# Order of one GpSimd multiply and two others in the steps that begin a row of chunks: gated linear attention followed by a mixture of experts, on one core

## The chip, the cores and the metric

The kernel runs on one core of one Trainium2 chip. The metric is the device time of one execution in microseconds (us). A core has five instruction streams that run beside each other and wait for one another by semaphores: TensorE (PE; its weight loads are shown as PEld), VectorE (DVE), ScalarE (ACT), GpSimd (POOL) and SyncE (SP, which here issues most of the DMA transfers). Each stream is worked off in the order in which it was written.

## The reference

The first half is a recurrence over 768 time steps for 4 batches and 8 heads of width 48; its rows are then routed to one of 8 experts each, a two-layer network with a ReLU, weighted by the gate.

```python
for t in range(S):
    state = alpha[:, :, t, :, None] * state + np.einsum('bhd,bhe->bhde', k[:, :, t], v[:, :, t])
    y[:, :, t] = np.einsum('bhd,bhde->bhe', q[:, :, t], state)
...
expert_idx = np.argmax(logits, axis=1)
...
h = np.maximum(x_sorted[lo:hi] @ w1[e], 0.0)
y_sorted[lo:hi] = h @ w2[e]
...
return (gate_w[:, None] * y).astype(np.float32)
```

## The kernel before

Time is cut into 6 chunks of 128 steps. One tile is one chunk of one batch: 24 tiles, numbered s = 4 * chunk + batch (`B` is 4). A step of the main loop (line 669, `for i in range(-4, NT)`) works on several tiles at once: it scores tile i, prepares the operands of tile i + 2, transposes those of tile i + 1, and projects tile i - 1. The whole loop stands under a manual schedule, so every engine runs its instructions in the order in which this loop writes them.

What a step writes, with the names and lines used below:

- **Loads** (`loads_for`, line 379): SP fetches a, k, q and v of later tiles, in pairs of tiles from step 2 on.
- **Scores** (line 461, PE) of tile i, then in steps 4, 8, 12, 16 and 20 `decay_cols` (line 429, PE): it transposes the row `er`, the decay that lies between two chunks, and DVE copies it to a tile `E` (line 431).
- **Masks** (line 469, DVE), **transposes** (line 448, PE) of tile i + 1, which read the tile `kqb`, **sums** (line 392, PE) with the two exponentials `icp` and `cp` (lines 395 and 396, ACT) of a tile further on.
- **Decay rows**: ACT issues small transfers of rows of `icp` and `cp` (line 409). In the steps before 4, 8, 12, 16 and 20 POOL makes `er` from them (lines 417 and 418).
- **`operands(i + 2)`** (line 438, POOL): two multiplies, k times `icp` and q times `cp`, into one of three tiles `kqb`. The tile is used again after `keys_values` (line 509, PE) of the tile before has read it.
- **`scale_state`** (line 476, POOL): the decayed state `U`, which is the state of the same batch one chunk earlier times `E`. In a step with i % 4 = 0 the state of tile i and that of tile i + 1 are both made there. In other steps only that of tile i + 1 is, except in the last of a row, where `decay_rows` stands in its place.
- **One-hots** (lines 290 and 291): the routing of earlier tiles, a pair of instructions for each tile, on POOL in steps 13, 14, 16, 19, 20 and 21 for tiles 0 to 10 and 13, and on DVE for others.
- **`read_state`** (line 488, PE) of tile i reads `U` of tile i; then `attend` (line 498), `keys_values` (line 509) and the projection `rows` of tile i - 1 (line 535), all PE. `rows` writes a PSUM tile `x` that ACT reads in `keep_rows` (line 560).
- In step 21, between `attend` and `rows`, PE sums up the routing of tiles 0 to 15 with 16 small matmuls, one for each tile in order (`tokens`, line 298). Their result is decoded on DVE and starts a gather on POOL (line 639) for the first expert rows.

After the loop the experts run one after another, with PE nearly without a gap.

Every transfer signals its completion on one of eight counters, and a transfer is not issued before the one that used its counter last has landed; which counter each takes is decided when the program is built.

Of the kernel before, what the change touches and what calls it, by code (L numbers as in the profile page):

```python
# [18 lines left out]
def kernel(  # L19
# [268 lines left out]
    def one_hots(eng, *tiles):  # L288
        for s in tiles:
            eng.tensor_scalar(oh_r[:, s, :], iota_r[:], scalar1=rc[:, 0, s : s + 1], scalar2=None, op0=ALU.is_equal)  # L290
            eng.tensor_scalar(
                oh_c[:, s, :], iota_c[:], scalar1=rc[:, 1, s : s + 1], scalar2=tokv[:, s : s + 1],
                op0=ALU.is_equal, op1=ALU.mult,
            )

    def tokens(tok_ps, *tiles):
        for s in tiles:
            nc.tensor.matmul(
                tok_ps, lhsT=oh_r[:, s, :], rhs=oh_c[:, s, :], start=(s == 0), stop=(s == NT - 1), skip_group_check=True,
            )  # L300
# [62 lines left out]
    with tc.tile_pool(name="ld", bufs=6) as ld, \  # L363
# [21 lines left out]
        def logs(s):  # L385
            t = work.tile([C, Dm], F32, name="lna", bufs=4)
            nc.scalar.activation(t[:], st[s]["a"].rearrange("s h d -> s (h d)"), AF.Ln)
            st[s]["lna"] = t

        def cums(s, bank="cum"):  # L390
            cum = ps.tile([C, 512], F32, name="cum", tag=bank)
            nc.tensor.matmul(cum[:, :Dm], lhsT=cum_m[:], rhs=st[s]["lna"][:], start=True, stop=True)  # L392
            cp = work.tile([C, Dm], F32, name="cp", bufs=6)
            icp = work.tile([C, Dm], F32, name="icp", bufs=6)
            nc.scalar.activation(icp[:], cum[:, :Dm], AF.Exp, scale=-1.0)
            nc.scalar.activation(cp[:], cum[:, :Dm], AF.Exp)  # L396
            st[s]["cp"], st[s]["icp"] = cp, icp

        def decay_out(s, which=(0, 1)):
            c, b = cb(s)  # L400
            cp, icp = st[s]["cp"], st[s]["icp"]


            for j in which:
                cc, row = ((c, icp[0:1, :]), (c + 1, cp[C - 1 :, :]))[j]
                if 0 < cc < NB:
                    if cc not in decay:
                        decay[cc] = work.tile([B, 2, Dm], F32, name="dec", bufs=3)
                    nc.scalar.dma_start(decay[cc][b : b + 1, 1 - j, :], row)
            if b == 0 and c + 1 < NB and 1 in which:  # L410
                alpha0[c + 1] = work.tile([B, H, D], F32, name="alpha0", bufs=3)
                nc.sync.dma_start(alpha0[c + 1][:], alpha[:, :, (c + 1) * C, :])

        def decay_rows(c):
            t = by_half(er[:B])
            d = decay[c].rearrange("b i (a p d) -> b i a p d", a=2, p=NP)
            nc.gpsimd.tensor_tensor(t, d[:, 0], d[:, 1], op=ALU.mult)
            nc.gpsimd.tensor_tensor(t, t, alpha0[c].rearrange("b (a p) d -> b a p d", a=2), op=ALU.mult)
# [7 lines left out]
        def decay_cols(c):  # L426
            ep = ps.tile([C, NP, C], F32, name="ep", tag="cum")
            for p in range(NP):
                nc.tensor.transpose(ep[:, p, :], pair(er[:], p), ident[:])
            decay[c] = work.tile([C, NP, B], F32, name="E", bufs=2)  # L430
            nc.vector.tensor_copy(decay[c][:], ep[:, :, :B])
# [82 lines left out]
        def result(s):  # L514
            d = st[s]
            d["yT"] = work.tile([C, 2, 2, C], F32, name="yT")
            nc.scalar.copy(d["yT"][:], y[:, :, : 2 * C].rearrange("r g (j t) -> r g j t", j=2))  # L517
# [46 lines left out]
        def do(f, i, *a):  # L564
            if 0 <= i < NT:
                f(i, *a)
# [7 lines left out]
        def new_sums(i):  # L574
            return range(sums_to(i - 1) + 1, sums_to(i) + 1)
# [9 lines left out]
        def loads_for(i):  # L585
            for n in singly.get(i, ""):
                load_next(n, 1)
            if i > 1:
                for n, upto in ("a", sums_to(i + 4)), ("v", i + 3), ("k", i + 5), ("q", i + 5):
                    while loaded[n] <= min(upto, NT - 1):  # L590
                        load_next(n, 2)
# [22 lines left out]
        def early_turn():  # L614
            t = ld.tile([C, 2, H, D], F32, name="k_sb", bufs=3)
            eg["xT"] = t.rearrange("p b h d -> p (b h d)").rearrange("p (a t) -> p a t", a=DB)
            for j in range(EARLY // C):
                tp = ps.tile([C, DB, C], F32, name="tp", bufs=2)
                for a in range(DB):
                    nc.tensor.transpose(tp[:, a, :], eg["xg"][:, j, a * C : (a + 1) * C], ident[:])  # L620
                nc.scalar.copy(eg["xT"][:, :, j * C : (j + 1) * C], tp[:])
# [11 lines left out]
        def early_gather():  # L633

            d = decode(held["tok"][:, : EARLY // C], EARLY // C, "e")
            gi = next(d)
            eg["xg"] = ld.tile([C, 2, H, D], F32, name="a_sb", bufs=4).rearrange("p j h d -> p j (h d)")
            for j in range(EARLY // C):
                nc.gpsimd.indirect_dma_start(
                    out=eg["xg"][:, j, :], out_offset=None,  # L640
                    in_=x_d[: (NG - 1) * TG * C, :], in_offset=bass.IndirectOffsetOnAxis(ap=gi[:, j : j + 1], axis=0),
                )
            return d
# [19 lines left out]
        def route(i):  # L663
            for f, *args in on_vector.get(i, ()):
                if f is slots:
                    args[1] = counted(args[1])
                f(*args)

        for i in range(-4, NT):
            loads_for(i)  # L670
            do(scores, i)
            if i < NT - 1:
                do(result, i - 1)
            do(logits, i - 2)
            if i >= B:
                do(add_state, i - 1)
            do(gate, i - 2)
            if i > 0:
                for s in new_sums(i):
                    logs(s)  # L680
            if i == NT - 1:
                early_turn()
            if 0 < i < NT and i % B == 0:
                decay_cols(i // B)
            do(mask, i, 0)
            do(mask, i, 1)
            if i < B:
                do(add_state, i - 1)
            do(transposes, i + 1)
            sums = list(new_sums(i))  # L690
            for s in sums[:1]:
                cums(s)
            if i < 0:
                for s in sums[1:]:
                    cums(s, "x")
            do(gate_weight, i - 2)
            route(i)
            do(keep_rows, i - 2)
            if len(sums) == 1:
                decay_out(sums[0])  # L700
            if i == -1:
                for s in range(2):
                    decay_out(s)

            if B - 1 <= i < 2 * B - 1:
                decay_out(i + 1, (1,))
            if i == NT - 2:
                si = next(se)[1]
                eg["si"] = lambda j, r: si[:r, j : j + 1]
            do(operands, i + 2)  # L710
            if i % B == 0:
                do(scale_state, i)
            if 0 < i + 1 < NT and (i + 1) % B == 0:
                decay_rows((i + 1) // B)
            elif i >= 0:
                do(scale_state, i + 1)
            one_hots(nc.gpsimd, *on_gpsimd.get(i, ()))
            do(read_state, i)
            do(attend, i)
            if i == NT - 2:  # L720
                result(i)
            if i >= 0 and sums[1:]:
                cums(sums[1])
                for s in sums:
                    decay_out(s, (0,) if i else (0, 1))
            do(keys_values, i)
            if i == NT - 3:
                held["tok"] = ps.tile([C, NC], F32, name="tok", tag="cum")
                tokens(held["tok"][:], *range((NG - 1) * TG))
                se = early_gather()  # L730
            do(rows, i - 1)
            if i in counts_in:
                counts(counts_in[i], counted(i - 1))
            if i < 0:
                for s in new_sums(i + 1):
                    logs(s)
            if i == -3:
                second_consts()
            if i in (-4, 0, 1):
                for j in {-4: (0, 1, 2), 0: (3,), 1: (4,)}[i]:  # L740
                    late_consts(j)
            if 12 <= i < 22:
                fetch_part(groups[0], i - 12)
# [515 lines left out]
```

## Time and profile before

| | us |
|---|---|
| median of 3 runs | 417.67 (416.52 to 418.47) |
| the profiled execution | 418.46 |
| its span, first to last instruction | 416.7 |
| PE busy | 404.7 (97%) |
| DVE busy | 208.8 (50%) |
| ACT busy | 171.2 (41%) |
| POOL busy | 144.2 (35%) |
| mean granted TensorE clock | 0.992 |

A share of the span says how long an engine had an instruction in it, not that it was needed that long. The loop with the 24 tiles fills the first third of the span, the experts the rest. A step takes about 5.45 us, one that begins a row of chunks about 5.9 us.

### The profile page before, as it was taken

To read this page: it belongs to the slowest core of one execution; us is meant where nothing else is said; L and a number is where in the kernel's file an instruction comes from. 1 tells how busy PE (TensorE), PEld (TensorE's weight loads), DVE (VectorE), ACT (ScalarE), POOL (GpSimd) and SP (SyncE) were. 2 spreads that over 40 slices of the span, in tenths; PEclk is the share of its full clock that TensorE was granted. 3 is DMA by queue.
4 is the path that set the end of the run, shared out by engine and by line. 5 is a ranking of instruction groups with operands and counts; after the bars stand their busy time and mean duration, and the time that the engine had idled before them with its cause. 6 is when DMAs were issued, how large, how long until landed. Compare 5 with 4: busy or idle time off the path is not lost.

```text
span 416.7 us, 9225 instructions
## 1 busy us (share of the span) xinstructions
PE 404.7 (97%) x3525; PEld 342.3 (82%) x3525; DVE 208.8 (50%) x644; ACT 171.2 (41%) x453; POOL 144.2 (35%) x193
## 2 busy tenths in 40 slices
PE   7997999999999999999999999999999999999994
PEld 4676888888888885999699889979979979979962
DVE  4552556464565575645743663463573573553200
ACT  4573565566655531134225414513513513523510
POOL 5545364678668204604002511320330230200101
PEclk9998999999999999999999999999999999999998
DMA  9999699889874316764405235155154263200101
GB/s 175 191 207 234 135 232 221 186 190 208 196 196 128 110 40 235 259 217 149 166 2 190 87 146 171 42 208 168 42 209 134 75 206 112 95 1 20 33 20 35
DMA packets 120098, 59.08 MB, mean 142 GB/s; under 512 B 102934, under 2 KB 114287, under 8 KB 120052
## 3 DMA queue, kind: packets, MB, share of 16 engines
q1 hardware_dynamic: 114932, 48.80, 45.3%
q0 software_dynamic: 3424, 9.59, 6.6%
q8 instruction: 29, 0.48, 0.5%
q10 hardware_dynamic: 1696, 0.08, 0.3%
q14 instruction: 17, 0.14, 0.1%
HBM read 48.95 MB, written 9.58 MB: 140 GB/s over the span
## 4 chain that ended last, share of the span: by engine, by line
PE 91%; issue 5%; ACT 1%; POOL 1%; DVE 1%; ACTq 0%; POOLq 0%
PE pA L884 11%; PE pB L884 9%; PE pC L957 8%; PE pA L942 7%; PE sA L461 6%; PE y L498 6%; PE tp L448 6%; PE cum L392 4%; PE pC L884 4%; PE x L535 4%; PE pB L942 4%; PE y L488 3%; PE pA L1096 3%; PE pC L942 2%; PE tp L800 2%
## 5 line engine op out<-in xcount | busy, mean ns | idle before, releaser
L979 POOL DMA_INDIRECT out_dram<-zo,sp x25 | 27.0, 1081 | 169.8 <-ACT zo L978 114.7
L184 DVE TENSOR_TENSOR h_sb<-pB,u 128x208 f32<-128x208 f32 (+6 forms) x56 | 20.1, 360 | 60.9 <-PE pB L884 44.9
L828 ACT COPY u<-pA 128x208 f32<-128x208 f32 (+6 forms) x68 | 21.6, 318 | 54.0 <-PE pA L942 50.3
L438 POOL TENSOR_TENSOR kqb<-k_sb,icp 128x384 f32<-128x384 f32 x23 | 23.0, 1002 | 42.5 <-PE y L509 21.0
L957 PE MATMUL pC<-h_sb,w 128*128 128x416 f32 (+5 forms) x96 | 32.9, 496 | 0.0
L884 PE MATMUL pA<-t,s 128*128 128x208 f32 (+6 forms) x112 | 28.6, 337 | 0.6
L461 PE MATMUL sA<-qT,kT 48*128 48x128 f32 x192 | 27.7, 284 | 0.9 <-DVE qT L452 0.9
L790 POOL DMA_INDIRECT xg<-x_rows,gp x25 | 25.9, 1036 | 7.6 <-issue 5.8
L957 PEld LDWEIGHTS pC<-h_sb,w 128*128 128x128 f32 x96 | 18.1, 190 | 12.0 <-issue 4.4
L461 PE MATMUL sB<-qT,kT 48*128 48x128 f32 x192 | 27.7, 285 | 0.0
L884 PE MATMUL pA<-xgT,w 128*128 128x208 f32 (+6 forms) x112 | 27.7, 329 | 0.0
L461 PEld LDWEIGHTS sA<-qT,kT 48*128 48x128 f32 x192 | 23.1, 187 | 3.8 <-ACT kT L454 1.1
L448 PE MATMUL tp<-ident,kqb 128*128 128x128 f32 x192 | 26.1, 279 | 0.0
L542 DVE TENSOR_REDUCE lgn<-x 128x8 f32<-128x32 f32 x23 | 4.4, 191 | 41.6 <-PE x L535 36.7
L448 PEld LDWEIGHTS tp<-ident,kqb 128*128 128x128 f32 x192 | 20.9, 141 | 3.3 <-issue 1.1
L884 PE MATMUL pB<-t,w 128*128 128x208 f32 (+6 forms) x112 | 23.4, 331 | 0.3 <-DVE h_sb L184 0.3
L438 POOL TENSOR_TENSOR kqb<-q_sb,cp 128x384 f32<-128x384 f32 x23 | 23.1, 1006 | 1.0 <-ACT cp L396 0.9
L897 ACT ACTIVATE h_sb<-h_sb 128x416 f32<-128x416 f32 (+6 forms) x28 | 14.8, 530 | 20.4 <-DVE h_sb L184 20.4
L884 PE MATMUL pC<-xgT,w 128*128 128x208 f32 (+6 forms) x112 | 23.1, 329 | 0.0
L461 PEld LDWEIGHTS sB<-qT,kT 48*128 48x128 f32 x192 | 23.1, 187 | 0.0
L469 DVE TENSOR_TENSOR dA<-sA,cmask 128x512 f32<-128x512 f32 x24 | 16.5, 689 | 11.4 <-PE sB L461 11.3
L517 ACT COPY yT<-y 128x512 f32<-128x512 f32 x24 | 14.1, 586 | 19.0 <-PE y L509 14.6
(252 smaller groups left out, 967.2 us busy)
## 6 DMA issues: line engine op xcount, KB each, us to landing
w<-in_moe_w_dram SPq DMA_DIRECT2D x14, 1536.0 KB, 7.5
x_rows<-xs SPq DMA_DIRECT2D x24, 192.0 KB, 3.8
v_sb<-in_v_dram SPq DMA_DIRECT2D x10, 384.0 KB, 5.4
k_sb<-in_k_dram SPq DMA_DIRECT2D x9, 384.0 KB, 6.7
q_sb<-in_q_dram SPq DMA_DIRECT2D x9, 384.0 KB, 6.2
a_sb<-in_alpha_dram SPq DMA_DIRECT2D x8, 384.0 KB, 4.7
a_sb<-in_alpha_dram SPq DMA_DIRECT2D x8, 192.0 KB, 4.0
w<-in_moe_w_dram SPq DMA_DIRECT2D x6, 256.0 KB, 3.0
```

Source lines behind the costliest of these rows:

```text
L184: eng.tensor_tensor(out, a, b, op=ALU.add)
L392: nc.tensor.matmul(cum[:, :Dm], lhsT=cum_m[:], rhs=st[s]["lna"][:], start=True, stop=True)
L438: eng.tensor_tensor(by_half(kq[:, i]), d[n].rearrange("s (a p) d -> s a p d", a=2), d[e][:].rearrange("s (a p d) -> s a p d", a=2, p=NP), ...
L448: nc.tensor.transpose(tp[:, p, :], pair(kqb[s % 3][:, i], p), ident[:])
L461: nc.tensor.matmul(t[:, p, :], lhsT=d["kT"][r : r + D, p, :], rhs=d["qT"][r : r + D, p, :], start=True, stop=True,)
L498: nc.tensor.matmul(yv(g)[o : o + D, j, :], lhsT=d["v"][:, g * NP + p, :], rhs=d["d" + "AB"[g]][:, p, :], start=(s < B and j == 0), stop=Tr ...
L790: nc.gpsimd.indirect_dma_start(out=g["xg"][:r, j, :], out_offset=None, in_=x_d[:, :], in_offset=bass.IndirectOffsetOnAxis(ap=g["gi"](j, r) ...
L828: nc.scalar.copy(t[:, :m], bank["A"][:, :m])
L884: nc.tensor.matmul(out, lhsT=ops[n_][0], rhs=ops[n_][1], start=first and n_ == names[0], stop=True, skip_group_check=True,)
L942: nc.tensor.matmul(out, lhsT=lhs, rhs=rhs, start=first and f == 0, stop=True, skip_group_check=True)
L957: nc.tensor.matmul(d2[:, :n], lhsT=w2[:, f, 2 * C :], rhs=h[:, f, :n], start=(f == 0), stop=(f == FB - 1),)
L979: ins = nc.gpsimd.indirect_dma_start(out=out[:, :], out_offset=bass.IndirectOffsetOnAxis(ap=g["si"](j, r), axis=0), in_=zo[:r], in_offset= ...
```

## The change

One line of the loop moves by two lines. In steps 4, 8, 12, 16 and 20 POOL ran both multiplies of `operands(i + 2)`, then `U` of tile i and `U` of tile i + 1. Now `U` of tile i stands first, then the two multiplies, then `U` of tile i + 1. In step 0 `scale_state` does nothing, since there is no earlier chunk, and in all other steps nothing moves.

```diff
             if i == NT - 2:
                 si = next(se)[1]
                 eg["si"] = lambda j, r: si[:r, j : j + 1]
-            do(operands, i + 2)
             if i % B == 0:
                 do(scale_state, i)
+            do(operands, i + 2)
             if 0 < i + 1 < NT and (i + 1) % B == 0:
                 decay_rows((i + 1) // B)
             elif i >= 0:
                 do(scale_state, i + 1)
             one_hots(nc.gpsimd, *on_gpsimd.get(i, ()))
```

In the built programs no instruction is added or taken away on any engine, and the order on PE, DVE, ACT and SP is the same. Two things differ beside the order on POOL. The semaphore that a `read_state` of such a step waits for now comes with the first `U` and no longer after the operands; the transposes of the next tile get a wait of their own for the operands. And from step 4 on the transfers take other completion counters than before, so that a load or a decay row can wait for another transfer than it did.

## The prediction

> **What bounds the kernel.** I read the slices first.
>
> ```profile
> PE   7997999999999999999999999999999999999994
> ...
> PEclk9998999999999999999999999999999999999998
> ```
>
> PE is busy nearly everywhere; slice 4 (31.3 to 41.7 us) is the one after the start with a dent, and the granted clock dips in the same slice. Next, PE's waits, longest first:
>
> ```profile
> PE y L488 <- POOL U L476: 2.5, 1, 2.5
> ```
>
> Columns: microseconds in total, times, longest. PE's largest wait in the whole span is one wait of `read_state` for `U`. The view of PE's weight loads shows five such waits, 5.0 us, the longest 3.1, but the load queue runs ahead: in steps 8, 12, 16 and 20 the matmuls have no gap. So what counts is step 4. POOL there, by its timeline (start, length, engine, line, what; in brackets the idle time before it and its releaser):
>
> ```profile
> 34.10 1.00 POOL L438 TENSOR_TENSOR kqb<-k_sb,icp 128x384 f32<-128x384 f32 x1 [1.37 <-DMA k_sb<-in_k_dram]
> 35.96 0.99 POOL L438 TENSOR_TENSOR kqb<-q_sb,cp 128x384 f32<-128x384 f32 x1 [0.86 <-ACT cp L396]
> 36.91 0.99 POOL L476 TENSOR_TENSOR U<-acc,E 128x192 f32<-128x192 f32 x2
> ```
>
> and PE:
>
> ```profile
> 34.15 0.81 PE L392 MATMUL cum<-lna,cum_m 128*128 128x384 f32 x2
> 37.48 0.65 PE L488 MATMUL y<-qT,U 48*48 48x128 f32 x16 [2.52 <-POOL U L476]
> ```
>
> Both multiplies of tile 6 wait for loads: k by the releaser named; q, I take it, also, since the `cp` of tile 6 was made two steps earlier (the `cp` that ended at 35.93 is tile 9's) and its load, issued at 30.36 with a median landing of 6.2 us, was due about then. `U` of tile 4, whose `E` DVE finished at 33.65, stands behind them. After the gap PE runs slowly. The windows (length, then busy time of PE, PEld, DVE, ACT and POOL; last three columns granted clock, DMA share, GB/s):
>
> ```profile
> 37.50:41.80 4.30, 4.30 (x66) 3.96 (x66) 0.00 (x0) 0.59 (x1) 1.50 (x3) 0.60 1.24 234
> ```
>
> In windows of half a microsecond the clock is 0.50 from 38.5 to 41.5 and 1.00 again from 42.0.
>
> **What step 4 gains.** `U` of tile 4 can start as soon after `E` as in step 8 (60.08 to 60.17, 0.09): at 33.74, and ends at 34.26 (row median 0.518). PE is then still in its transposes and sums, so `read_state` follows the sums as elsewhere, 0.74 behind their start (60.59 to 61.33): 34.89 in place of 37.48, which is 2.59 us. From there to the next scores step 8 takes 61.33 to 64.01 = 2.68 us at full clock, step 4 took 37.48 to 41.79 = 4.31: another 1.63. Together **4.22 us**. As a check: from scores to scores step 4 took 31.64 to 41.79 = 10.15, step 8 58.13 to 64.01 = 5.88, a difference of 4.27.
>
> [...] The row shows half clock 0.7 us after that gap, for some 3.4 us. [...]
>
> What is late next? `rows` of tile 3 would stand at 34.89 + 1.85 (61.33 to 63.18) = 36.74; it needs `x`, which ACT's `keep_rows` frees at 36.40 (35.82 + 0.58): 0.34 to spare. The transposes of tile 6 come 1.09 after the scores (64.01 to 65.10), at 38.7; its q multiply still starts with the load at 35.96 and ends at 36.95. `U` of tile 5 ends at 37.4 and is read at 40.4. None of these takes the gap's place.
>
> **Steps 8, 12 and 16.** [...] POOL in step 8 now:
>
> ```profile
> 57.62 1.00 POOL L438 TENSOR_TENSOR kqb<-k_sb,icp 128x384 f32<-128x384 f32 x1 [0.30 <-issue]
> 58.58 1.01 POOL L438 TENSOR_TENSOR kqb<-q_sb,cp 128x384 f32<-128x384 f32 x1
> 60.17 0.99 POOL L476 TENSOR_TENSOR U<-acc,E 128x192 f32<-128x192 f32 x2 [0.59 <-DVE E L431]
> ```
>
> The operands fill the time in which POOL would wait for `E`. With `U` first POOL idles until 60.17, and behind it the operands end at 60.17 + 0.50 + 1.92 = 62.59 in place of 59.58, 3.01 later. [...] The rows say who waits: the transposes of tile 10 start at 65.10, 2.51 later. The second `U` ends at 63.09, read at 66.77. The next operands (63.51) wait for PE anyway, and POOL had 2.35 us idle there. Cost 0. Step 12 has the same offsets (`U` 82.93, operands to 85.35, transposes 87.87, next operands 86.27). In step 16 two tiles of one-hots follow (2.13 us), so the next operands start at 110.20 instead of 108.50; their transposes stand at 116.07, and POOL's idle 3.00 before 113.93 takes the delay up. Cost 0. If those covers were gone, each step would cost up to its 3.0 less whatever is left.
>
> **Steps 20 and 21** have no such cover:
>
> ```profile
> 125.90 1.00 POOL L438 TENSOR_TENSOR kqb<-q_sb,cp 128x384 f32<-128x384 f32 x1
> 127.27 0.99 POOL L476 TENSOR_TENSOR U<-acc,E 128x192 f32<-128x192 f32 x2 [0.37 <-DVE E L431]
> ...
> 130.37 1.00 POOL L438 TENSOR_TENSOR kqb<-k_sb,icp 128x384 f32<-128x384 f32 x1
> 131.32 1.02 POOL L438 TENSOR_TENSOR kqb<-q_sb,cp 128x384 f32<-128x384 f32 x1
> 132.28 0.53 POOL L476 TENSOR_TENSOR U<-acc,E 128x192 f32<-128x192 f32 x1
> 132.78 0.65 POOL L290 TENSOR_SCALAR oh_r<-iota_r,rc 128x128 f16<-128x128 f16 x1
> 133.41 0.48 POOL L291 TENSOR_SCALAR oh_c<-iota_c,rc,tokv 128x32 f16<-128x32 f16 x1
> ```
>
> From 127.27 to 133.89 POOL has no gap. The operands of tile 22 (1.92) now fall behind the first `U`, so all that follows is 1.92 later: operands of tile 22 done at 129.69 (transposes 131.26, fine), `U` of tile 21 at 130.19 (read at 132.29, fine), operands of tile 23 at 134.2 (transposes 136.34, fine), `U` of tile 22 at 134.7 (read 137.36, fine), but the one-hots of tile 13 at 135.8. PE wants them here:
>
> ```profile
> 133.88 0.56 PE L298 MATMUL tok<-oh_c,oh_r 128*128 128x32 f16 x16
> ```
>
> Tile 13 is the fourteenth of these: 133.88 + 13 * 0.033 = 134.31. PE stops until 135.87: **1.55 us lost**. Everything behind (projection, decode, gather, next steps) hangs on PE's order or on this sum and shifts with it. Bounds: 0 if POOL packs tighter, 1.55 + 1.63 = 3.2 if the stall brings half clock as in step 4. [...]
>
> **The transfers.** Counters change from step 4 on, so waits for landed transfers change. The tightest I find: ACT's row of `icp` in step 6 now waits for the q load of tiles 8 and 9, issued at 37.80, largest landing 6.9: 44.7, against 50.69 - 4.2 = 46.5 when ACT gets there. In return the k load of tiles 10 and 11, held until 50.73 by a decay row, is freed. k of tiles 12 and 13 waits for a decay row issued at about 51.9 (56.12 - 4.2): + 3.6 + 6.7 = 62.2, its multiply 64.7. Cost 0; from below nothing to gain, since PE waits for no load after step 4; from above the 4.2 could be handed back. The ten added waits of the transposes: the row is the 51 ns semaphore instruction, 14 times before `read_state` with no gap on PE; 0, at most 10 * 0.05 = 0.5.
>
> **Sum.** -4.22 + 1.55 = -2.67. The profiled execution, 418.46 (span 416.7 and 1.8 around it), goes to 415.8. It is 0.79 above the median 417.67; taken from that, 415.0. The spread of the three runs, 1.95, is about a clock dip, so some may lack it, and a run without it gains less but starts lower. I take 415.3, 0.57% under the median.
>
> **The rivals.**
> - *As summed*, 0.55: 415.3.
> - *No stall in step 21*, 0.13: 417.67 - 4.2 = 413.5. For: POOL's spans are rough. Against: POOL is packed for 6.6 us there.
> - *Half the clock's part is missing*, 0.24: the median run had no dip, or step 21 gets one: -2.6 + 1.55 = -1.05 or -4.2 + 3.2 = -1.0, so 416.7. [...] Against: two of three runs sit high.
> - *Loads take the gain back*, 0.08, the other side: with step 4 shorter, the DMA-bound start (share 1.24, 234 GB/s) or a counter holds a load of steps 6 to 11 until PE waits for it. Price: one for one beyond the slack of 1.8 us at ACT and some 4 at the transposes; it decides once 4.2 is handed back and the stall stays: 417.67 + 1.55 = 419.2, more if it comes twice. For: SP issues of 1.4 to 2.9 us until 42. Against: share 0.5 from 42 to 46.
> - *The change does nothing* is ruled out: POOL's order differs in five places.
>
> About 0.5% (2.1 us) is what a measurement of this kernel can tell from no change. Faster: most of the first and the second, 0.61; within: the third and the edges, 0.33; slower: the tail of the fourth, 0.06. The range 413.3 to 417.1 holds the first three.
>
> **What would show it.** PE's wait for `U` of 2.5 gone, slice 4 of PE and clock at 9, step 4 at about 5.9 us; POOL idle for `E` some 2 to 3 us in steps 8, 12, 16, 20 with no gap on PE; a new PE wait at L298 for POOL's one-hots near 1.5. A wait of PE for a load, or a clock under 1.00 after step 21, would make me wrong.

## The result, and the profile after

| | before | after |
|---|---|---|
| median of 12 runs, us | 417.62 (416.21 to 418.47) | 416.62 (415.39 to 418.75) |
| ratio, 95% interval | | 0.9982 (0.9962 to 1.0001) |
| the profiled execution, us | 418.46 | 415.39 |
| its span, us | 416.7 | 413.7 |
| mean granted TensorE clock | 0.992 | 0.997 |

By the medians the change gains 1.0 us, 0.24%, which the interval does not separate from nothing. A gain of 0.57% was forecast. The two profiled executions are 3.07 us apart, close to the 2.67 of the sum, but by luck: the one of before is the second highest of its twelve runs, and the one of after the lowest of its twelve. That is the first thing to see here: the trace that the sum was read from was not a typical one. Here and below, ratios leave out runs more than 1.5% above the fastest of their kernel (two of e2, one of e3), while medians hold all runs.

The slices of after, beside the dent in slice 4 of before:

```profile
PE   7999999999998999999999999999999999999994
...
PEclk9999999999999999999999999999999999999998
```

The dent is gone, in PE and in the clock. A new one stands in PE's slice 13. PE's waits of after (us in total, times, longest) name it:

```profile
PE tok L298 <- POOL oh_c L291: 1.4, 1, 1.4
```

The wait for `U` is off the list. POOL's timeline of after, step 4 first (start, length, engine, line, what; in brackets the idle time ahead and its releaser):

```profile
33.46 0.51 POOL L476 TENSOR_TENSOR U<-acc,E 128x192 f32<-128x192 f32 x1 [1.00 <-DVE E L431]
34.04 1.00 POOL L438 TENSOR_TENSOR kqb<-k_sb,icp 128x384 f32<-128x384 f32 x1
35.64 1.00 POOL L438 TENSOR_TENSOR kqb<-q_sb,cp 128x384 f32<-128x384 f32 x1 [0.61 <-DMA q_sb<-in_q_dram]
...
122.77 0.51 POOL L476 TENSOR_TENSOR U<-acc,E 128x192 f32<-128x192 f32 x1 [2.27 <-DVE E L431]
...
130.71 0.47 POOL L291 TENSOR_SCALAR oh_c<-iota_c,rc,tokv 128x32 f16<-128x32 f16 x1
```

In step 4 `U` no longer stands behind the q multiply, which still waits for its load until 35.64. In step 20 POOL now idles 2.27 us for `E`, and the queue behind it ends with the one-hot of tile 13 in step 21, at 131.18. PE's timeline of after, in steps 4 and 21:

```profile
34.62 0.65 PE L488 MATMUL y<-qT,U 48*48 48x128 f32 x16
...
129.39 0.49 PE L298 MATMUL tok<-oh_c,oh_r 128*128 128x32 f16 x13
131.24 0.23 PE L298 MATMUL tok<-oh_c,oh_r 128*128 128x32 f16 x3 [1.36 <-POOL oh_c L291]
```

`read_state` has no gap ahead of it (2.52 us before), and the token sums stop ahead of tile 13 for 1.36 us. So both halves of the sum are in the trace. What they are worth in other executions is what the experiments had to find.

### The profile page after: what moved, and what is told of

It reads as the page before. It is cut to its first block, busy times and chain, and to the rows that moved or that the text cites. A ratio compares the mean times of both kernels' runs of the same rounds, so it can differ in the third digit from the quotient of the medians.

```text
span 413.7 us, 9238 instructions
## 1 busy us (share of the span) xinstructions
PE 402.2 (97%) x3525; PEld 340.5 (82%) x3525; DVE 213.2 (52%) x644; ACT 171.1 (41%) x453; POOL 143.7 (35%) x193
## 4 chain that ended last, share of the span: by engine, by line
PE 86%; issue 6%; POOL 4%; ACT 2%; DVE 1%; DMA 0%; POOLq 0%; ACTq 0%
PE pA L884 11%; PE pB L884 9%; PE pC L957 8%; PE pA L942 8%; PE sA L461 5%; PE tp L448 5%; PE y L498 5%; PE pC L884 4%; PE pB L942 4%; PE cum L392 4%; PE x L535 4%; PE pA L1096 3%; PE pC L942 2%; PE y L488 2%; PE tp L800 2%
## 5 line engine op out<-in xcount | busy, mean ns | idle before, releaser
L187 DVE TENSOR_TENSOR th<-h_sb,th 128x208 f32<-128x208 f32 (+5 forms) x48 | 17.4, 363 | 7.9 <-ACT h_sb L897 7.9
```

The costliest lines, as they stand in the source:

```text
L187: eng.tensor_tensor(out, a, b, op=ALU.subtract)
```

## The experiments

The runs fall in three groups of four kernels, each group on one chip. The kernel before took 420.82 us (median of 35 runs) in the first group, 417.28 (29) in the second, 421.39 (29) in the third. Ratios are to the runs of before in the same group.

The reading used throughout is a table: from PE's timeline of each trace, the time from the first score product of step 4 to that of step 10. In steps without any wait this stretch takes 33.55 us, as it does in e8 (steps of 5.88, 5.45, 5.44, 5.45, 5.88 and 5.45). What is above that is lost to waits and to half clock.

| trace | PE's wait for `U` in step 4 | half clock after it | step 4 to step 10 | lost |
|---|---|---|---|---|
| before | 2.52 | yes | 37.82 | 4.27 |
| before, e1 | 1.84 | no | 35.82 | 2.27 |
| old order in step 4, e4 | 2.10 | no | 35.71 | 2.16 |
| before, e12 | 2.14 | yes | 37.33 | 3.78 |
| old order, decay rows moved, e11 | 1.89 | yes | 37.10 | 3.55 |
| after | 0 | no | 33.59 | 0.04 |
| after, e2 | 0 | no | 34.50 | 0.95 |
| new order in step 4, e3 | 0 | no | 35.03 | 1.48 |
| new order, e5 | 0 | no | 34.37 | 0.82 |
| new order, e9 | 0 | no | 34.66 | 1.11 |

The table leaves out what PE loses ahead of step 4. That matters for the old order, since a PE that comes late to step 4 can wait less there: step 3 took 5.83 us in e1 and 6.16 in e4, in the other traces 5.23 to 5.73. From the first scores of step 0 to those of step 10 the five traces of the old order take 59.56 us in the mean, the five of the new 56.96.

### e1 and e2: both kernels again

No edit.

> The kernel before, unchanged, for a second trace of it. Theory A (the sum of the prediction holds in every execution): PE waits again about 2.5 us for U in step 4 and runs at half clock after it, mean granted clock 0.992. Theory B (the profiled execution was an extreme one: PE comes to step 4 earlier or later while the load that U stood behind lands at a time of its own, so that the wait swallows what the start lost): the wait is shorter here, 1 to 2 us, most executions show a mean clock of 0.995 or more, and scores of step 5 start near 41 us whatever the start was. Ratio 1.000 by both.

> The changed kernel, unchanged, for a second trace and more times. Both theories: ratio 0.998, no wait for U in step 4, PE stops 1.4 us at the token sums of step 21. Theory B adds: the executions of this kernel spread wider than those of the kernel before (3.4 against 2.3 us so far), because the start's lateness is no longer swallowed, and a longer execution is longer before step 4 already.

Measured: before 421.15 us, ratio 1.0011 (0.9986 to 1.0037); after 420.80, ratio 1.0001 (0.9968 to 1.0035). PE's timeline of e1, and the clock's slices of its page:

```profile
37.23 0.65 PE L488 MATMUL y<-qT,U 48*48 48x128 f32 x16 [1.84 <-POOL U L476]
```

```profile
PEclk9999999999999999989999999999999999999999
```

The wait is 0.68 us shorter than in the first trace of before, and slice 4 of the clock is a 9. The trace of after has no wait for `U`, but loses 0.95 us in steps 4 to 7: `er` came 0.24 late in step 4, and steps 5 and 6 took 5.80 and 5.74 us in place of 5.45. In the 12 runs of each, the change gains nothing here.

### e3 and e4: the two halves alone

e3 moves `U` ahead in step 4 only, e4 in step 20 only (`i == 5 * B`).

```diff
+            if i == B:
+                do(scale_state, i)
             do(operands, i + 2)
-            if i % B == 0:
+            if i % B == 0 and i != B:
                 do(scale_state, i)
```

> The first U ahead of the operands in step 4 alone; steps 8, 12, 16 and 20 as before. Theory A: 4.2 us less than before, ratio 0.990. Theory B: what the change brought, 1.0, plus the stall of step 21 that this kernel doesn't have, 1.4: 2.4 us less, ratio 0.9943. Both: no stall at the token sums.

> The first U ahead of the operands in step 20 alone. Both theories: the stall of 1.4 us at the token sums of step 21 and nothing else, ratio 1.0033. If the stall were swallowed later, 1.000; if it brought half clock in most executions, 1.006.

Measured: e3 419.76 us, ratio 0.9973 (0.9944 to 1.0003). e4 422.88 us, ratio 1.0042 (1.0008 to 1.0075). By the ratios step 4 alone gives 1.1 us, a quarter of the 4.22, and at most 2.4 by the interval; step 20 alone costs 1.8 us, 0.3 to 3.2 by the interval, which holds the 1.55. In the trace of e4 the stop at the token sums is 1.36 us, in e3 there is none. The two ratios multiply to 1.0015, which the interval of e2 holds; steps 8, 12 and 16, which neither of them has in the new order, need no cost of their own. In no trace has PE a gap in steps 12 or 16, and in step 8 only in e3 and e9, where `er` is late.

### e5: one one-hot earlier

The changed kernel, with the one-hots of tile 13 in step 19, in the time in which POOL would wait for `E`.

```diff
-... 4 * B + 3: (8,), 5 * B: tiles(9, 2), 5 * B + 1: (13,)}
+... 4 * B + 3: (8, 13), 5 * B: tiles(9, 2)}
```

> The changed kernel with one thing more: GpSimd makes the one-hots of tile 13 in step 19, in the idle time ahead of the first U of step 20, and not behind the second U of step 21. Theory A (the sum holds in every execution: step 4 gives 4.2 us, only the stall at the token sums takes some back): ratio to the kernel before 0.990. Theory B (the loads pace the start, step 4's wait is 1.8 to 2.1 us in most executions and has no dip of the clock, and 0.5 to 1.0 us of it comes back as waits of the running sums and of the decay rows in steps 5 to 9): ratio 0.9955, between 0.994 and 0.998. Both: no wait at the token sums, unless VectorE's one-hots of tile 15, which ended 0.4 us before GpSimd's in the trace of after, turn out to be late by themselves; then a wait of 0.9 us is left, and the ratio 0.002 higher.

Measured: 415.97 us, ratio 0.9976 (0.9955 to 0.9996). PE's timeline of e5:

```profile
131.75 0.18 PE L298 MATMUL tok<-oh_c,oh_r 128*128 128x32 f16 x1 [0.54 <-DVE oh_c L291]
```

POOL's one-hot no longer stops PE, VectorE's of tile 15 does, for 0.54 us. Behind one late producer stood a second, whose wait the first had hidden.

### e6: a longer gap in step 4

The kernel before, in which POOL multiplies q of tile 6 twice.

```diff
             do(operands, i + 2)
+            if i == B:
+                do(operands, i + 2, (1,))
             if i % B == 0:
                 do(scale_state, i)
```

> The kernel before, but GpSimd does the q multiply of tile 6 twice in step 4, so that the first U comes 0.96 us later and PE's gap is 2.8 to 3.1 us in place of 1.8 to 2.1. Theory A (the gap's length decides the clock, and 2.5 us is enough): half clock for some 3.4 us after it in slice 4, so that scores to scores of steps 4 and 5 take 10.5 to 11 us. [...]

Measured: one execution of 419.35 us. The line numbers of this kernel are shifted by two. PE's timeline, and the clock in the window after the gap (length, then busy time of PE, PEld, DVE, ACT, POOL; granted clock, DMA share, GB/s):

```profile
38.34 0.82 PE L490 MATMUL y<-qT,U 48*48 48x128 f32 x16 [3.30 <-POOL U L478]
```

```profile
38.30:42.60 4.30, 4.25 (x64) 3.76 (x64) 0.00 (x0) 0.59 (x1) 1.23 (x2) 0.60 1.05 201
```

A gap of 3.30 us, a step of 11.0 us, and half clock (0.60 in the mean of this window), as Theory A has it. One gap of this length does not show that the length decides; the table shows that it does not, where waits of 1.89 and 2.14 had the dip and 2.10 had not.

### e7 and e8: PE late by itself

Eight products that nobody reads, ahead of the scores of step 3, in the kernel before (e7) and in the changed one (e8).

```diff
+            if i == 3:
+                late(8)
             do(scores, i)
```

> The kernel before, with eight more 128-column products on PE ahead of the scores of step 3, into the bank that those scores write next and whose result nobody reads: about 1.9 us of PE's time. Theory A (PE's order sets the time at the start): 1.9 us longer, ratio 1.0045, and the gap of step 4 stays at 1.8 to 2.5 us. Theory B (the arrival of the q load sets the end of the gap in step 4): the gap shrinks by 1 to 1.9 us, and the ratio is 1.000 to 1.002.

> The same eight products ahead of the scores of step 3 in the changed kernel. Theory A: 1.9 us longer than the changed kernel, so 1.9 minus 2.7 against the kernel before: ratio 0.998. Theory B: there is no gap in step 4 that could take them up, but with PE later the waits of steps 5 to 9 (0.5 to 1.0 us) go: 0.9 to 1.9 us longer than the changed kernel, ratio to the kernel before 1.001 to 1.004.

Measured: e7 416.95 us, ratio 1.0001 (0.9987 to 1.0014). e8 418.33 us, ratio 1.0029 (1.0012 to 1.0047). From the scores of step 2 to those of step 3 PE takes 7.98 and 7.99 us in the two traces in place of 5.88, so the products cost it 2.1 us there. In the kernel before that costs nothing at the end. POOL's and then PE's timeline of e7:

```profile
35.48 1.01 POOL L438 TENSOR_TENSOR kqb<-q_sb,cp 128x384 f32<-128x384 f32 x1 [0.81 <-DMA q_sb<-in_q_dram]
36.45 0.99 POOL L476 TENSOR_TENSOR U<-acc,E 128x192 f32<-128x192 f32 x2
```

```profile
37.02 0.66 PE L488 MATMUL y<-qT,U 48*48 48x128 f32 x16
```

The load of q ends POOL's wait at 35.48, inside the span in which it does in the other traces of the old order (35.13 to 36.10), and `read_state` starts at 37.02 as in e1 (37.23) and e12 (37.02), now without a gap that the wait list names. The gap was PE's lead over that load. With PE late there is no lead, and the change has only its cost left: e8 is 1.4 us slower than e7.

e8 shows the token sums' stop at its worst. PE's timeline, and the window behind it:

```profile
133.15 0.23 PE L298 MATMUL tok<-oh_c,oh_r 128*128 128x32 f16 x3 [1.39 <-POOL oh_c L291]
```

```profile
134.00:138.00 4.00, 4.00 (x42) 3.31 (x42) 2.73 (x10) 1.33 (x4) 2.69 (x3) 0.61 0.29 72
```

The clock is at one half from 134.9 to 138.3, after a gap of 1.39 us, and step 22 takes 5.98 us in place of 4.42. The three other traces with this stop (1.36, 1.36 and 1.40 us) kept full clock.

### e9: both one-hots earlier

As e5, with tile 15 moved too, from VectorE to POOL.

```diff
-... 5 * B + 1: [(one_hots, nc.vector, 15)], ...
-... 4 * B + 3: (8,), 5 * B: tiles(9, 2), 5 * B + 1: (13,)}
+... 4 * B + 3: (8, 13, 15), 5 * B: tiles(9, 2)}
```

> The changed kernel with the one-hots of tiles 13 and 15 both made by GpSimd in step 19, ahead of the first U of step 20; VectorE no longer makes those of tile 15. If the two late one-hots are all that stops PE at the token sums (GpSimd's of tile 13, then VectorE's of tile 15 with 0.55 us), there is no wait left there, and the ratio to the kernel before is 0.55 us lower than the 0.9976 of the version with tile 13 alone: 0.9963, between 0.994 and 0.998. By the prediction's sum (4.2 us in step 4, nothing handed back) it would be 0.990.

Measured: 419.88 us, ratio 0.9956 (0.9928 to 0.9983). The token sums have no wait, step 21 takes 5.07 us as before. With nothing given away in step 21 the new order gains 1.9 us (0.44% of 421.39; 0.7 to 3.0 by the interval), not 4.2.

### e10 and e11: the decay rows

What the new order hands back in steps 5 to 9 is seen best in e9. ScalarE's timeline (ACTq is its issue of transfers), then PE's:

```profile
41.15 0.51 ACTq L409 DMA_DIRECT2D dec<-icp  x1
41.74 2.16 ACTq L409 DMA_DIRECT2D dec<-cp  x2
43.95 0.59 ACT L517 COPY yT<-y 128x512 f32<-128x512 f32 x1 [2.28 <-DMA dec<-cp]
44.73 0.51 ACT L387 ACTIVATE lna<-a_sb 128x384 f32<-128x384 f32 x1
```

```profile
45.29 0.91 PE L392 MATMUL cum<-lna,cum_m 128*128 128x384 f32 x2 [0.28 <-ACT lna L387]
...
55.90 0.66 PE L429 MATMUL ep<-ident,er 128*128 128x128 f32 x4 [0.48 <-POOL er L418]
```

Two issues of decay rows take 2.16 us (1.19 in the trace of after), the copy of `yT` and the logarithm `lna` behind them start later, and PE comes to its sum first; in step 8 it comes first to `er`. The other traces agree: where such a pair of issues in steps 4 to 6 took 1.86 to 2.33 us, the next step took 5.60 to 5.99 us in nine of ten cases, in both orders; where it took 1.18 to 1.83, the next step took 5.44 or 5.45 us, but for one with a dip of the clock. e10 is e9 with the second of these rows, for tiles 4, 5 and 6, written a step later behind the logarithm; e11 is that move in the kernel before.

```diff
+            if B <= i < 2 * B - 1:
+                decay_out(i, (1,))
             do(transposes, i + 1)
...
-            if B - 1 <= i < 2 * B - 1:
+            if i == 2 * B - 2:
                 decay_out(i + 1, (1,))
```

> As the version with both one-hots early, and the decay rows of tiles 4, 5 and 6 for the chunk after next are issued on ScalarE's queue one step later, behind the logarithms and ahead of the copy of kT, where before they stood ahead of the copy of yT. Theory B1 (ScalarE's issue of these rows, which took up to 1.5 us in place of 0.6, makes the copy of yT, the logarithms and so PE's running sums late in steps 5 to 7, and that is where 0.8 us of step 4's gain is handed back): those waits go, steps 5, 6 and 7 take 5.45 us each from scores to scores, ratio 0.994, between 0.992 and 0.997. Theory B2 (the loads themselves are late, and the issue only waits with them): the waits stay or move to the logarithms, and the ratio is that of the version with both one-hots early.

> The same move of the decay rows in the kernel before. Theory B1: step 4's gap is set by the load of q and swallows what PE gains ahead of it; only the 0.36 us of step 6 in one of three traces of the kernel before goes. Ratio 0.999 to 1.000. By the prediction's sum (no cost at the transfers): 1.000.

Measured: e10 419.23 us, ratio 0.9942 (0.9914 to 0.9970), 2.4 us faster than before. e11 421.10 us, ratio 0.9989 (0.9959 to 1.0020). ScalarE's timeline of e10 in the same step:

```profile
41.26 0.50 ACTq L409 DMA_DIRECT2D dec<-icp  x1
41.85 0.55 ACTq L409 DMA_DIRECT2D dec<-cp  x1
42.64 0.59 ACT L517 COPY yT<-y 128x512 f32<-128x512 f32 x1 [0.56 <-PE y L509]
43.80 0.55 ACTq L409 DMA_DIRECT2D dec<-cp  x1
```

`yT` starts at 42.64, 0.24 us after the two issues ahead of it end, and its releaser is PE; steps 5 to 9 take 5.44, 5.45, 5.45, 5.88 and 5.45 us, with no wait. In this trace the 0.44 us that it does lose come in step 4, where `er` was 0.37 late. So the place and the path are shown in the traces. That the move is what helped is not shown: the trace of after lost nothing in these steps either, and by the times e10 and e9 are not apart, their intervals overlap. Why an issue sometimes takes long (in e5 up to 1.51 us at a median of 0.55) was not tried; one guess is the completion counter, since a load of SP stood up to 4.2 us for a decay row in the trace of before (`SPq L379 <- DMA dec<-cp: 6.2, 4, 4.2`). In the kernel before the move is worth nothing that can be measured, which fits a lead over q's load that swallows it.

### e12: one more trace of before

No edit.

> One more trace of the kernel before. Theory A (2.5 us of wait and a dip of the clock in step 4 as in the profiled execution): steps 4 to 10 take 37.8 us from scores to scores. [...]

Measured: one execution of 420.74 us. PE's timeline, and the clock's slices:

```profile
37.02 0.66 PE L488 MATMUL y<-qT,U 48*48 48x128 f32 x16 [2.13 <-POOL U L476]
```

```profile
PEclk9998999999999999999999999999999999999999
```

A wait of the middle size, with the dip this time. Of the five traces of the old order in step 4 at PE's own pace, three have it. In the second group, 15 of the 29 runs of the kernel before had a mean clock of 0.997 or more; a dip, 3.4 us at half clock in a span of some 415 us, leaves 0.996 at most. So there it came in no more than 14 of 29. The dip is no rule, and five traces do not say how often it comes.

## Why the prediction came out as it did

**Where the change acts was right.** The wait for `U` goes, POOL idles for `E` in the steps that begin a row, steps 8, 12 and 16 cost nothing, and a new wait of PE for the one-hot of tile 13 appears in step 21. It was put at 1.55 us; the gap is 1.36 to 1.40, and step 21 grows by 1.51 to 1.55. No load made the kernel slower than before.

**The first term of the sum failed: "Together 4.22 us".** It is the loss of one execution. Over the five traces of the old order the loss in steps 4 to 10 is 3.2 us in the mean (2.16 to 4.27), since the wait is 1.84 to 2.52 and the half clock is there or not. The prediction took the one gap that it had seen with a dip, 2.52 us long, for the usual case, and gave an execution without the dip a quarter of the chance; of the five traces three have it and two have not. The experiments bear it out: with the cost of step 21 out of the way, e9 gains 1.9 us and e10 2.4. A profiled execution 0.8 us above the median of three was a hint that its own losses were above the usual.

**The second failure is the line "The transfers ... Cost 0".** The five traces of the new order in step 4 lose 0.04 to 1.48 us in the same steps, 0.88 in the mean, which the sum did not have. PE waits there for sums and decay rows that ScalarE and POOL get late, in steps 4 to 9. It is a relative of the fourth rival, at a fifth of its price: a transfer takes gain back, but in no trace does PE wait for a load in these steps; what comes late hangs on the issues of the decay rows. The gain in steps 4 to 10 then is 3.21 less 0.88, 2.3 us, in place of 4.2; counted from step 0 it is 2.6.

**A third term was a little small.** The stop in step 21 has its own dip in one of four traces: 1.5 three times and 3.1 once, 1.9 in the mean, beside the 1.8 of e4. The prediction held 3.2 as its upper end and took the value without a dip, which was its author's estimate.

2.3 less 1.9 is 0.4 us, and 2.6 less 1.9 is 0.7, between the 1.0 of the first comparison and the 0.0 of e2, whose intervals both hold it. The third rival had the time of the first comparison, 416.7, in part by luck, and half of the reason: the size of the dips. The other half was its neighbour's.

**What was mistaken in the way of reading.** The wait of 2.52 us was taken as a cost of the queue's order, with a size of its own. e7 shows that it was the distance between PE and a load that lands when it lands: 2.1 us of added work on PE went into it without trace. A wait of that kind varies with what stands ahead of it (1.84 to 2.52 us in the five traces), and what is saved there can meet the next transfer.

## What to carry to other kernels

A wait at the end of a stretch that is fed by loads can be a lead, not a price (in e7 2.1 us of added work cost nothing): ask what PE meets next if it does not wait here, and read the wait from several executions before it goes into a sum. A reordering on a full queue pays for what it moves back (here 1.36 to 1.40 us at the token sums); look for the idle time that it opens on the same engine (here 2.27 us ahead of the first `U` in step 20) and put the displaced work there, as e9 did, which made 0.4% of a change that alone gave nothing certain. When one late producer is moved, look at the others of the same consumer: here the second still held it for 0.54 us.

## What the runs showed of the hardware

**Half clock after short gaps, by where they fall.** Gaps of PE of 1.39, 1.89, 2.14, 2.52 and 3.30 us were followed by some 3.4 us at a granted clock of 0.50; gaps of 1.36, 1.36, 1.40, 1.84 and 2.10 were not. The length alone does not decide. The clock records of the traces show what else does. Within a trace, all changes of the clock lie whole multiples of 3.413 us apart: in that of before half clock begins at 38.21, ends at 41.63, and begins again after PE's last work at 413.68, 110 times 3.413 after the first; in e8 it begins at 134.85 and again at 414.75, 82 times 3.413 later. Against the kernel this raster lies elsewhere from execution to execution: it has borders at 38.21 and 41.63 us in before, at 36.20 and 39.61 in e1. Of the gaps with a dip, one stretch of the raster held 1.39 us of idle PE (e8), 1.88 (e11), 1.92 (e12), 2.52 (before) and 3.06 (e6), and half clock began at its end. In e1 and e4 a border of the raster cut the gap; the two stretches of e1 (length, then busy time of PE first):

```profile
32.79:36.20 3.41, 2.60 (x24) 1.86 (x20) 2.55 (x7) 2.50 (x7) 1.50 (x2) 1.00 0.98 215
36.20:39.61 3.41, 2.38 (x60) 2.20 (x62) 0.00 (x0) 0.94 (x3) 1.65 (x4) 1.00 1.22 240
```

So 0.81 and 1.03 us of idle PE fell into them, in e4 0.66 and 1.43. Over the 14 traces, from 12 us on, every stretch at full clock with 1.47 us or more of idle PE was followed by half clock (but for one of 1.91, in which PE's work ends in e6), none with 1.36 or less was, and from 1.38 to 1.44 both occur. This was read from the traces afterwards; no run was made to test it. For a sum, a gap of 1.4 to 2.5 us in this kernel costs its length and, in four of nine such gaps, 1.56 (e8) to 1.75 us (before) more.

**Two engines that stop together.** In the first and third groups every trace has a stretch near 170 to 180 us, in the first expert, in which ScalarE stands still twice, for 3.55 and 3.97 us, and VectorE for 5.10 us (e1), both past the time at which PE has written what they read (in e9 VectorE stands 5.14 us and reads `pC` at 173.49, 4.90 us after PE's product for it ends at 168.59); PE then waits 1.9 to 2.4 us in pieces (e9 to e12), and in six of the eight traces the clock dips. The second group and the two first traces have none of it: in before ScalarE waits 1.40 us at the same places, and VectorE 0.28. There the kernel before takes 417.3 to 417.6 us, in the others 420.8 to 421.4. It strikes kernels of both orders alike. The DMA engines do not tell the cases apart: their share falls from above 1.0 to about 0.5 in both traces, in e1 at 170 us, as VectorE's stop begins. What holds the two engines was not tried.
